# A four-layer attention kernel whose recorded order, engine choices and PSUM banks are replaced by another set

## The chip, the cores and the metric

The kernel runs on one core of one Trainium2 chip. The metric is the device time of one execution in microseconds (us). A core has TensorE (PE in the profile), which multiplies matrices into PSUM, VectorE (DVE), ScalarE (ACT), GpSimd (POOL) and SyncE (SP), which here only issues transfers. Each engine plays its own list of instructions in order and waits on semaphores for the others. PSUM has eight banks; one bank holds 128 partitions by 512 float32.

## What is computed

The input x is [1, 2048, 512] in bf16. Four layers follow one another, each with a layer norm before it and a residual after it: A, B, A, B. There are 32 heads of 16 elements. A is linear attention, B is attention over a sliding window of 256 positions.

```python
def _A_ref(x, wqkv, wo):
    ...
    phi = lambda t: jnp.where(t > 0, t + 1, jnp.exp(t)) + 1e-6
    pq, pk = phi(q), phi(k)
    kv = jnp.einsum("bhsd,bhse->bhde", pk, v)
    z = jnp.einsum("bhsd->bhd", pk)
    num = jnp.einsum("bhqd,bhde->bhqe", pq, kv)
    den = jnp.einsum("bhqd,bhd->bhq", pq, z)[..., None] + 1e-6
    o = num / den
    return (lambda x, *d: x.transpose(*d))(o, 0, 2, 1, 3).reshape(B, S, D) @ wo

def _B_ref(x, wqkv, wo):
    ...
    scores = jnp.einsum("bhqd,bhkd->bhqk", q, k) * (Dh ** -0.5)
    mask = (idx[:, None] - idx[None, :] >= 0) & (idx[:, None] - idx[None, :] < W)
    scores = jnp.where(mask[None, None], scores, -1e9)
    p = _softmax(scores, axis=-1)
    o = jnp.einsum("bhqk,bhkd->bhqd", p, v)
    return (lambda x, *d: x.transpose(*d))(o, 0, 2, 1, 3).reshape(B, S, D) @ wo

x = x + _A_ref(_layernorm(x, axis=-1), A_wqkv, A_wo)
x = x + _B_ref(_layernorm(x, axis=-1), B_wqkv, B_wo)
x = x + _A_ref(_layernorm(x, axis=-1), A_wqkv, A_wo)
x = x + _B_ref(_layernorm(x, axis=-1), B_wqkv, B_wo)
```

## The kernel before

The 2048 rows are cut into 16 tiles of 128 rows. A Python class first writes down a graph of 2532 operations, one operation being one instruction or a short run of matmuls on one engine, with the data that it reads and writes and the PSUM tiles that it uses. The residual stream `xres` stays on the chip for all four layers.

A layer of kind A does, per tile: the norm (bn_stats L330, bn_aggr L331, two small POOL operations L332 and L333, and the normalised tile xn L334); a transpose of xn, either by a DMA (L340, issued from SP) or by TensorE into PSUM with a copy out (L346, L353); the products k and v (L369) and q (L383); phi, which is an exp on ScalarE (L392) and two VectorE operations (L393, L394). In the first layer the sums over the whole sequence are gathered by the operation g (L444), in the third by kv (L423). From these sums come the small matrices M (copied by L358), the denominators den (L506), their reciprocal (recf L510, recb L511), its spread over the rows (L519) and the scaling of q (pqd L526). Then per tile aout (L369 with M) and the residual (L537).

A layer of kind B does, per tile: the norm again, and bq, bk (L383) and bv (L369) from the transposed tile xT; copies out of PSUM (bqe L358 to XQ, bke L554 or L555, bve L358 to vS); two copies of the keys to `kB` by DMA (kd, L563) and two of the values to `vB` (vd, L582), all from SP; scores (L599) with exp on ScalarE (L609) and a mask on VectorE (mk L615); the part of the window that is two tiles away (scores L632, exp L641) with the mask mf, which can run on POOL (L649) or on VectorE (L650); the values product pv (L674), the reciprocal of the sums (rcp L685) and the division (div L686); a transpose of o (oT, by DMA or by TensorE L709), the output product bout (L369, for the last tile L720), and the residual (L537, for the last tile two halves L726). Tiles 0 to 14 of the last layer go out by a DMA from POOL (L783), the last tile by two from SP (L727).

Layer B of tile t needs the tiles around it alone, so neighbouring layers overlap: the front of layer 2 starts while layer 1 ends, and the norm and k of layer 3 run inside layer 2.

What sets the order is no planner that runs at build time, but a recorded table. `TABLE` (L796 to L852) is a compressed string. `place()` unpacks it into three things: one global order of all operations, the engine of each operation, and the bank of each of 997 PSUM tiles. Each engine's instruction list is the global order cut to that engine. Where a PSUM tile takes a bank, its first operation waits for all users of the tile that held the bank before:

```python
order = [ops[raw[2 * k] + 256 * raw[2 * k + 1]] for k in range(n)]
...
o.eng = ("PE", "ACT", "DVE", "POOL", "SP")[raw[2 * n + o.i]]
...
x.banks = [raw[3 * n + k]]
...
before = held[x.banks[0]]
if before:
    assert all(u.t0 < o.t0 for u in before.users)
    o.deps.extend(u for u in before.users if u not in o.deps)
held[x.banks[0]] = x
```

`synchronise()` then turns the dependencies into semaphore waits, with a ring of 48 semaphores for the transfers from SP. `run()` plays the order on each engine. On TensorE it starts with nine matmuls on zeros whose result nobody reads (they go to bank `SPARE`), and `FILL` (L857) puts further ones behind chosen operations: two behind the first, one behind the fourth, six behind the sixth.

Of the kernel before, what the change touches and what calls it, by code (L numbers as in the profile page):

```python
# [11 lines left out]
P = 128  # L12
D = 512
DH = 16
S = 2048
T = 16
# [196 lines left out]
class Plan:  # L213
# [579 lines left out]


TABLE = (
    r"c-rk(1Jq?nlFo<>WR`8)wr$(CZQHhO+qP|2wQYCpd+)ER>6z)7?d|Q|b9PU~|G&KV2EL5=B3_<%jfrF;8#GZ(6a&T@Hqi{3=q9BR6T`$bsZ44U",  # L796
    r"%cL=}O&pWf#5L)Rnmi_+NpJF+_@=$dVDg##CZkDUI+#JGqse3{nyIFk>0}C+X(qENXq-uCN}435kntv|8Emqc#wMKEX_}bCX1SSenwo4TndxkX",
    r"m>Fh;X=b{ZT_(IaZL*uLCWk3yikrgbuIXlSn&zgv*=_EbnI@6xVa}LbW|qlnhMJY;7gNr(Fsn>YGt8VdtIcq8-?TKn%tvO88DYws(xxPwGb7C?",
    r"6B&w_*=CO!ZO)rH=2w&4d~7b52d0l1W9FK@rnebuJ~1!NJ~PjJYSx;EX1-ZxN|<q`j7bXX%_FnGj5h{0n9s~YlMFVRYUXou(PW29X1^(GqQGU7",
    r"!W=N0%@vaz4w_OB6|S1crZhY;Dd3O+Xbgu<4TG@BJT*tmQIis)!58M4Nd>u0eRJJBHx*13^QCEJu9+9+D^tmof#_i2YZC)<Kuz<FA!uzFaza^n",  # L800
    r"$FwoIpd1J^fp1M)lN(ZlLLHL_(m*>?*QAB-jDrZKDWrqSCOyQ2dL|b1HMLD_=x5?Ud8lRjo48N`JWPa&kQWA+d=MWhK~Xc%#Do0M$Yg{JP#Gqe",
    r"MP{)n01Zq*SYir6LsJ+gnn`A<X$F&EnW+jbpbFH5de9MS!(_9?R5w#h9jI!ynodw3wwVUd5E{XD(;1GL=FkOpn3m8Ux<M;w3+<pQw1(rR4RnAT",
    r"=7i}1lVJ*UhovwTmcdDL2ByKg<}56SZE({}hf`(-yl1w<Ot@uMz${n^=U_Ihg73|0m;*bYC%kVKz#7;IYhfWAhudZm?1Emf8&1F;SPXOFB-}Cc",
    r"Afo9FKbXBRAI?J`*attFjnEG^!8-WBEP<cQX1D--;Ua{CQ*a4BH0vQ8{%peIWe5-b;R;m12rvK+!3H=C5g`I@fk$uzDq<vf0!Lv#RKf#r8XiML",
    r"{1C3fRyYVB!$)uzjzJ`>jFIskM8Rut1*771xDTH~G`xzR!&A5cpFkD73D@v5cnDST8C1htFbN;P3#g8h@eX_e@o@@1hZL9quVX5Vj_*JXjDZO;",
    r"B__d`*bozAGQ5F}a4O!0FJT}w#-un62f@4W6*R@^7z<}$226yhF*e@BjF=p6;d_t?;$SAs4DZ8COoLy;Ec^hnKwA6;vfyAyhjlP3WX1IO6V%0Q",
    r"P!qFZW^9J_uogDK7ML9uV{Kf5&G9yN!ljr4?_g)li7oMG$c0_-7s!pRups^lv#~YK!I$t9+u&UM7M`KOt{4vizlXbs_#ETnJ^T(VcEkHP4+(qV",
    r"4=^7KVO#8udGJRljP)@eR)Zqg0INe@EQ;;0J=TB)xB_cJ0w{((u{f^64p;ygYk}ZO?1%}W1S+n<)z}O3<610<z0qMQT!#;^5B9}Gum#uSVBCO-",
    r"VJmLKB(M=ZF2jeo376w$e1t<_JC??wPzIyfvKZYChY?T?ci=E60y{B=9fIX?DDJ|dFbs>qhZxh=wjbectYc%@;TYTQ!H+SH9f8GRFV?jq@mm~)",
    r"`*4AcYrn@55YH~O`|&%hXWzx-_9%XW@8Kdl8sEo$xY$0mi*Skk0Y}18`wrH(&ujxb3I<?*Y-q<|3LD>kfXi%3`y~#<WB4^bw}bFFCa_=O2|R#}",  # L810
    r"?5B7TM?+(~+<t?fVM2QdGuY4ZG5&}zY({$+U*Jjn2{YLz_ywl1@7SMlEWT?O;xCxij>98pZF74HGu!ca8gtn9Y&zS*PQcW5BA&sVHkD0p6WRA|",
    r"V%yT@vU%)T%wm(+y!ISswfSsEo6R<{*=;AA+cvfNE!k$av+ZixcC!Vn*e<raJ&$TH;IG)jUc`bnnSF_uu#LTpZLP6|th0S>Ve4%>8_t%r8*P6J",
    r"c9ZRA2U@i4ZFt+$4zerk0K3`tvV-k5o7DEUrR;V)#73~CZ6CYCma)6+P}{+lwY%*a`++TIciOeKyxn6f*dlhF9cGK#y>_J?ZY$bi_K+Q6E7?`{",
    r"h>d7V*wr?Y9cK^QG4Q1=ZpT7o`<2~lCqOFt+HSF_X*{&D<KURBY+KtX_JmDCRcusS)sD2s?T5CSU2m(~kL(6J+NP!Pc7jbuAKRlgJ)N@??I@dp",
    r"+EWM0NEhrR`-#m&pW2i5yxnIf+p%_vooe^nj`W%R$zHNw*aP;IJ!pTno#?dv#eQec*ex{8cBb#`S-X|G(69Eg%}rzMHu}NlAxn8F8%?)NUFk=g",
    r"ox0IWOLWoZpl__wb~4nR9POaYw3C25Wg(<p^tlx(Kw0UE{ni$ut2P|Xum$OwooS2Ebvw(3r=oPj&bBvg1e#-S*<w_IBGNY$i3(Fi>P^L|58bwv",
    r"s0`h)ed${&OC{(#ia{l*GL@t6X(;ue;gpZcQ&0MVO3{y$pLSCf8b&`+Y3fB)X(UynyS6%wrV(_{)}@~*CXJ$46q)YZ*ffB0QWSb%2hu}(l=e_m",
    r"8brq^4o#)wRF4MJ7@9_LDH_G2TvVSP+4wY_hENT9Y!gsTicSe>u5Cc`Y%MxK4XHmJr1`cEO{9L*hz`+Mnnb_Q6FZI?(+rwSP3RPjr@b_RPSX@h",
    r"MEmFrC8qs!j*?JQnn`Er0yU$gG>ekadAdcj3HT(<q1%Lfkrq*H61IGYu95Nyx<Sq9E;(*N*Xa^nrj~S*!gDKHOjjr(U!^6~nj&yyUP||98Aav$",
    r"w4Czs3W~xHXeGtwhm@Zq@pFp9tLRrMz%MB-&!yF5I62Luc$|WwaU1eHpHfnMK0<9N0WYMpe3;tNIZnur=mjkx=Ew97CE{?rhTf$ow3dk9qxX3o",  # L820
    r"CFc(~I<Kdc{60OS4RoGUa18!{I&n<?kUr$%9E(5V#9We}(#M>HOK@RM%}Kc+cjjbVgwyaf?!wo(D3{{${1I)W3j8q@<4shWEAnP4!-Y5%-{8tz",
    r"mM?H6uFB>3BH!dHe2IJWE$+kB_!GL#pHg4$&T08G>c>6#bNYnS@fXyCKjrjXoj>Cm+>0~taPG?e`Ewr0HTer3z#}*#*Wye(m<MtL&dguZARfx2",
    r"_$$i7mw5<(O<8#<U*Y9k!w%zRT${V`3a)9davdJcb$JXo<gr}KHsXa`pU3fH9?xI$B5ustxE^QcCY*ztGRQ`5#$WMf&dJSr32$PQuek-U<=p%Y",
    r"uj7`yh4b)w{+1_jUf#eHITugj?|3VJ&y#r@ujC*2N1no~cq(t_X}p75@oH|*cX&Fl;TilB-{pI}ldUwD`@D-E@NVA2E#x8Z<<|U&_i-DZ$1}MD",
    r"&*#UypWE^QCOOE5cow(g!#tax@DYB>3z+37pW<UYhv)KfKF!a#BR}U8e3D=A8GeV~<@fk!ZYFspkNm>L<X0{t;ib4lkfQRE3rPtv5>Z47O96=_",
    r"`6RNGl>DMnN(zdT($Z2|Nf~J^V`ZGglr~aUdP^T^E90e|#FF;XSC&W==^*{2qb!w9;w7r|mkBaJVoNs}D9fa~Oq9+tNG3@S2`7VPvUHK2GDPA?",
    r"Ihi6|rI!qqxDri<NqLzn!)1g_laW$EmP<t$CDCQNtdJ_QQpU(CsVp;OmduvXGE*wae5oo6WR9$sW3o{0$Xq!gG32f+lC5%F?#VpaCEMh_ES5bI",
    r"MYqcuiK@Hhft-?u5=}plM{-)CYZ)!8XC#K6lusq5K9&z9mX^~e@|k=t@g%m!m-3oecF0GvRuV`Yt)Tm4uT<1^@`db|N}5nM$a>i+N#uZ>m8bHt",
    r"B$8*6R1V5Uc`lb^lN^#{a#*fNa@i~|<Q+L8Tja7Fl`rL8`9$LCR}xRJ%KLIouE}|cuV2fLazPU4Mfq7OYf`-~-$*k3NfK&uttN@|S4pYW#b_1%",
    r"R=$(8@{7Ebbn?BtCpDz5{vhcEG?k{%dYVB}Yeu;tH>JL&QPEq1npjoSs@1AW>NK6QR@3mBUTdh=>RMAXXf~~-Q#FT9(~KHUhv;<8u8nl4HqlI)",  # L830
    r"Q-^70ZLGsJmqySmnny=yR*k45b(E%%+!{$!%4jX5sU)wC(d?31a!6!NBl)z57S`IDUz=)9X{H6Vffm(F(n1?*X2~T5^|mC@+|pdzX&oJ_?X`op",
    r")Z%(pi|IH$r&*+?bky-$N6za6tt%6?mSmMqI!SBG9__5zWUqG761q=kX-VC$v-NW=rC;bA?W(=Bw0^1eq>oP416p6Y=@dPvy>*@*(yz3YF3`E!",
    r"TEEuA`i*wiBicZ|)%n^++v+m?PSdy*+Cyh(PfhC<Y7_UpF4umV&Rx=`F1@>=i?qM?)n;z7Ue*k5l`heln$aEAmAYCpxutqco4XUbMq9XRdR$w&",
    r"liJGN(5pH?*Xlq$rPp<n4$>d=jBe4J`lGgXr*)lXcAIsu{-pPGz24Vt`m=7(3;IBR(T#dhAL*|O?ul+!bhq@eS|=`xd#Jb7xu?2S^SV2#?yiP&",
    r"`CNGSO!K=o?zu*AwcHD3m({(awOvG)&3&Za?a(?dyL(r6D!KQxo{Qvmsd4XXEca5|x;U<#`%ojh_Aa*T=c2gXn!`nP{asGi)zx*m+yEENb#u|(",
    r"#~Rmtpxxak8p9=WpK1q}$0czcT}+qTeWvkTCzse2a`D|jSJ)+R1zl2C#1(S|TtZjEC3g*_s7vM=NpaU$=C~$O&dqgArMz3~=DBsQf-C8Ix%sY?",
    r">+Ke}^{%vA==!)tu97R`Qn=1;v8&=zy0UJG>+7z#RIaj{<gU7ku8T|Urno`wnj7pUyQ*%RyY8yF?QV!0>Z-dNZil<+M!BA@hP&mQuj$4(?{B-Q",
    r"ZmGND!uio|m|Nz;`w?!MTj6@R<!+@L?l!qqu87~_#=4?@wTs|Kx`_U%tM7KYNPe^1=Zg7f?tmNTwz}tTyxZ?0`*&S&AI0x-@3{%CgrDekyOREW",
    r"SISR!huj`_*X?zOU1@*M9dv7419#sYai`n{_knBZHoDU;sz2%)xoG~3`_?sf(fu*^y*uvCxd-k$cf!5nzH}$uL-)d+bzi#~?!0^CX1cH3hi;aO",
    r";XiVZ-48CN|Hj4jv)#uomjBho^Do^e?nhU~$M-)u<J0+{T^#?Z`^9DO=s$DmeIgG&f&bi9^<TKeKB2$hF1n2ViA&;>`Ag3FYCeT8>#O^6KDJNp",  # L840
# [12 lines left out]
)

FILL, SPARE = {1: 2, 4: 1, 6: 6}, 6  # L857


class Kernel(Plan):  # L860
# [153 lines left out]
```

## Time and profile before

| | us |
|---|---|
| median of four runs | 431.83 |
| lowest, highest | 431.75, 433.44 |
| the profiled execution | 431.78 |
| its span in the trace | 430.1 |
| outside the span | 1.68 |

The mean granted TensorE clock was 0.988 of full speed. The page cuts the span into 40 slices of 10.75 us; each digit is a busy share in tenths:

```profile
PE   8899999999899999999999999999899989998775
DVE  6998898998998799897887789988798687966474
ACT  2433547999899999999998255999999988999992
POOL 4789221101240233130403303212144414242000
PEclk9999999999999999999999999999999979999989
```

Layer 1 lies in about the first seven slices, layer 2 up to about slice 21, layer 3 in slices 20 to 27, where ScalarE is emptier, and layer 4 in the rest. In the clock's row a 9 is full speed; in two places, slice 33 and slice 39, it is lower. The costliest groups are read in this way: line, engine, operation, output and input with their shape, count; then busy time and the mean of one in ns; then the idle time of the engine just before them and what ended it.

```profile
L609 ACT ACTIVATE pb<-ps 128x1024 bf16<-128x1024 f32 (+2 forms) x224 | 207.2, 1041 | 8.9 <-PE ps L599 7.6
L674 PE MATMUL ps<-vB,pb 128*128 128x34 bf16 x2560 | 83.7, 178 | 2.5 <-DVE pb L615 0.6
L383 PE MATMUL ps<-xT,wBp 128*128 128x128 bf16 x1024 | 69.6, 219 | 2.2 <-DMA xT<-xn 1.5
L649 POOL TENSOR_SCALAR_AFFINE_SELECT pb<-pb 128x1024 bf16<-128x1024 bf16 x30 | 35.2, 1174 | 38.8 <-ACT pb L641 37.6
```

The exponentials of the scores are by far the largest group: 224 instructions of about a microsecond, 207.2 us on ScalarE, which sat idle for 8.9 us before them.

### The profile page before, as it was taken

The page shows a single profiled execution, that of the slowest core. Times are in us where ns is not written, and L with a number is a line of the kernel's source. Part 1 is how long each engine was busy: PE and PEld are TensorE (multiplying, and loading weights), DVE is VectorE, ACT ScalarE, POOL GpSimd, SP SyncE. Part 2 cuts the span into 40 slices and gives each one's busy share as a digit, 9 for nine tenths or more (in the row PEclk, how much of TensorE's full clock was granted, in tenths as well). Part 3 has the DMA queues.
Part 4 walks back from the last instruction along what each step waited for, and adds up shares of the span by engine and source line. Part 5 has one row for each costly group of instructions (what it writes and reads, how often), then busy time and mean ns, then how long its engine had stood idle before and what let it go on. Part 6 is the DMA issues. An engine that isn't in the chain of part 4 may idle for free.

```text
span 430.1 us, 17112 instructions
## 1 busy us (share of the span) xinstructions
PE 402.4 (94%) x7548; PEld 257.7 (60%) x7548; DVE 355.9 (83%) x796; ACT 347.5 (81%) x433; POOL 128.3 (30%) x223
## 2 busy tenths in 40 slices
PE   8899999999899999999999999999899989998775
PEld 3445676766465566565566768576657636665444
DVE  6998898998998799897887789988798687966474
ACT  2433547999899999999998255999999988999992
POOL 4789221101240233130403303212144414242000
PEclk9999999999999999999999999999999979999989
DMA  8833016433152533452315000552423622553321
GB/s 247 265 76 87 2 40 161 117 93 74 38 106 63 103 101 76 93 114 53 99 41 66 15 2 29 122 107 64 113 77 95 111 76 65 98 141 107 79 53 50
DMA packets 66978, 37.81 MB, mean 88 GB/s; under 512 B 48248, under 2 KB 61816, under 8 KB 66904
## 3 DMA queue, kind: packets, MB, share of 16 engines
q1 hardware_dynamic: 66176, 34.75, 35.0%
q0 software_dynamic: 720, 1.97, 1.3%
q8 instruction: 59, 0.97, 1.0%
q14 instruction: 15, 0.12, 0.1%
q10 hardware_dynamic: 8, 0.00, 0.0%
HBM read 6.29 MB, written 2.10 MB: 20 GB/s over the span
## 4 chain that ended last, share of the span: by engine, by line
PE 43%; ACT 33%; DVE 15%; DMA 4%; issue 3%; POOL 1%; SPq 0%; POOLq 0%; ACTq 0%
ACT pb L609 23%; PE ps L369 15%; PE ps L383 11%; PE ps L674 7%; ACT pb L641 5%; PE ps L599 5%; ACT vp L609 3%; DVE XQ L526 2%; DMA xT<-xn 2%; DVE stats L330 2%; DVE vp L394 2%; PE ps L444 1%; DVE tE L393 1%; DVE vp L334 1%; ACT tE L392 1%
## 5 line engine op out<-in xcount | busy, mean ns | idle before, releaser
L609 ACT ACTIVATE pb<-ps 128x1024 bf16<-128x1024 f32 (+2 forms) x224 | 207.2, 1041 | 8.9 <-PE ps L599 7.6
L674 PE MATMUL ps<-vB,pb 128*128 128x34 bf16 x2560 | 83.7, 178 | 2.5 <-DVE pb L615 0.6
L674 PEld LDWEIGHTS ps<-vB,pb 128*128 128x128 bf16 x2560 | 77.9, 96 | 13.5 <-issue 3.0
L392 ACT ACTIVATE tE<-ps 128x512 bf16<-128x512 f32 x64 | 39.0, 612 | 41.0 <-PE ps L369 20.7
L383 PE MATMUL ps<-xT,wBp 128*128 128x128 bf16 x1024 | 69.6, 219 | 2.2 <-DMA xT<-xn 1.5
L332 POOL TENSOR_SCALAR ve<-mv 128x1 f32<-128x1 f32 x64 | 16.5, 259 | 175.7 <-DVE mv L331 173.9
L383 PEld LDWEIGHTS ps<-xT,wBp 128*128 128x128 bf16 x1024 | 58.8, 98 | 14.8 <-issue 3.8
L615 DVE TENSOR_TENSOR pb<-pb,tri 128x512 bf16<-128x512 bf16 x112 | 48.0, 436 | 12.4 <-ACT pb L609 11.6
L599 PE MATMUL ps<-XQ,kB 32*128 32x256 bf16 (+2 forms) x1024 | 50.2, 271 | 8.2 <-ACT pb L609 3.9
L369 PE MATMUL ps<-wA,XQ 128*128 128x512 bf16 x192 | 49.3, 380 | 1.7 <-DVE vp L394 1.0
L641 ACT ACTIVATE pb<-ps 128x1024 bf16<-128x1024 f32 x50 | 49.3, 1057 | 0.9 <-PE ps L632 0.8
L537 DVE TENSOR_TENSOR xres<-ps,xres 128x512 bf16<-128x512 f32 x63 | 43.0, 685 | 7.7 <-PE ps L369 6.8
L649 POOL TENSOR_SCALAR_AFFINE_SELECT pb<-pb 128x1024 bf16<-128x1024 bf16 x30 | 35.2, 1174 | 38.8 <-ACT pb L641 37.6
L330 DVE BATCH_NORM_STATS2 stats<-xres 128x6 f32<-128x512 bf16 x64 | 43.1, 681 | 2.7 <-DMA xres<-in_A_x_dram 2.1
L333 POOL TENSOR_TENSOR rs<-ve,negh 128x1 f32<-128x1 f32 x64 | 37.5, 586 | 5.3
L369 PE MATMUL ps<-wBv,xT 128*128 128x512 bf16 x128 | 36.4, 389 | 0.6 <-ACT pb L609 0.4
L599 PEld LDWEIGHTS ps<-XQ,kB 32*128 32x128 bf16 x1024 | 15.5, 92 | 35.8 <-ACT pb L609 15.4
L369 PE MATMUL ps<-M,XQ 128*128 128x512 bf16 x128 | 35.3, 389 | 1.4 <-DVE XQ L526 1.3
L383 PE MATMUL ps<-XQ,wA 128*128 128x128 bf16 x512 | 36.1, 219 | 0.2 <-DVE vp L394 0.2
L383 PEld LDWEIGHTS ps<-XQ,wA 128*128 128x128 bf16 x512 | 30.6, 98 | 7.7 <-DVE vp L394 1.2
L369 PE MATMUL ps<-wBo,oT 128*128 128x512 bf16 x124 | 33.1, 382 | 0.8 <-ACT pb L609 0.6
L685 DVE RECIPROCAL rc<-ps 128x16 f32<-128x16 f32 x64 | 16.1, 252 | 17.0 <-PE ps L674 16.6
(109 smaller groups left out, 541.5 us busy)
## 6 DMA issues: line engine op xcount, KB each, us to landing
vB<-vS SPq DMA_DIRECT2D x64, 136.0 KB, 2.6
kB<-vp SPq DMA_DIRECT2D x64, 128.0 KB, 2.3
out_dram<-xres POOLq DMA_DIRECT2D x15, 128.0 KB, 2.6
wA<-in_A_wqkv_dram SPq DMA_DIRECT2D x3, 512.0 KB, 5.7
xres<-in_A_x_dram SPq DMA_DIRECT2D x2, 512.0 KB, 4.9
pb<-in_B_wqkv_dram SPq DMA_DIRECT2D x1, 1024.0 KB, 8.3
xres<-in_A_x_dram SPq DMA_DIRECT2D x3, 256.0 KB, 4.7
wAo<-in_A_wo_dram SPq DMA_DIRECT2D x1, 512.0 KB, 7.1
```

What stands on the lines that cost most here:

```text
L330: self.on("DVE", "stats", lambda e: e.bn_stats(K.stats[:, t, :], K.xres[:, t, :]), key, dve(512), rd=[("xres", t)], wr=[("stats", t)])
L333: self.pow = self.on("POOL", "pow", lambda e: e.tensor_tensor(K.rs[:, t, :], K.ve[:, t, :], K.negh[:], ALU.pow), key + 0.03, (640, 690), r ...
L369: m = e.matmul(K.ps(ps), lhs(c), rhs(c), start=c == 0, stop=c == 3)
L383: m = e.matmul(K.ps(ps)[:, f * P:(f + 1) * P], w(c, f), xT(c), start=c == 0, stop=c == 3)
L392: self.on("ACT", "E", lambda e: e.activation(K.tE[:, s, :], K.ps(ps), ACT.Exp, bias=0.0), key, act(512), wr=[("tE", s)], ps=[ps])
L537: self.on("DVE", "res", lambda e: e.tensor_tensor(K.xres[:, t, :], K.ps(po), K.xres[:, t, :], ALU.add), key, dve(512), rd=[("xres", t)], w ...
L599: m = e.matmul(K.ps(ps[gq])[:, ns * i:ns * i + ns], K.kB[rows, j % 4, 2 * f + b, :, :], K.XQ[rows, f, q:q + ns], start=True, stop=True, ti ...
L609: return e.activation(out(2 * h, 2, ns), i, ACT.Exp, bias=0.0, scale=0.25)
L615: return e.tensor_tensor(x, x, K.tri[:, 0, :].unsqueeze(1).unsqueeze(1).to_broadcast([P, 4, n, 64]), ALU.mult)
L641: return e.activation(far(h), i, ACT.Exp, bias=0.0, scale=0.25)
L649: return e.affine_select(out=x, in_=x, compare_op=ALU.is_ge, fill=0.0, base=-2, pattern=[[0, 16], [-2, 64]], channel_multiplier=1)
L674: m = e.matmul(K.ps(ps)[:, 34 * u:34 * u + 34], K.P((b // 2) % rp)[:, gq, f, o:o + P], K.vB[:, (b // 2) % 4, b % 2, r, :], start=i == 0, s ...
```

## The change

The operations, their dependencies through data and all instructions that compute are the same. The recorded table is another one, so that all of its lines differ, and one filling matmul is added behind the eighth operation of TensorE:

```diff
 TABLE = (
-    r"c-rk(1Jq?nlFo<>WR`8)wr$(CZQHhO+qP|2wQYCpd+)ER>6z)7?d|Q|b9PU~|G&KV2EL5=B3_<%jfrF;8#GZ(6a&T@Hqi{3=q9BR6T`$bsZ44U",
...
+    r"ALN64kPq@fK8P{@22lJcMg",
 )
...
-FILL, SPARE = {1: 2, 4: 1, 6: 6}, 6
+FILL, SPARE = {1: 2, 4: 1, 6: 6, 8: 1}, 6
```

Unpacked, the two tables differ as follows. "Moved" counts the operations that have another place among those which stay on their engine.

| engine | operations before | after | moved | farthest |
|---|---|---|---|---|
| TensorE | 858 | 858 | 179 | 10 places |
| VectorE | 795 | 797 | 338 | 17 places |
| ScalarE | 432 | 429 | 46 | 1 place |
| POOL | 219 | 220 | 70 | |
| SP | 228 | 228 | 124 | 5 places |

Of 997 PSUM tiles 117 have another bank. 24 operations change engine: eight masks mf go from VectorE to POOL and seven from POOL to VectorE; two bqe and one xT copy (L353) go from VectorE to ScalarE; one ge, two ve, two oTe (all copies out of PSUM) and one recb go from ScalarE to VectorE.

The moves on TensorE are dense in its first 130 operations (the first 60 us), around its operations 470 to 560 (about 230 to 267 us) and in its last ten. Single places that the text below speaks of, with the times that the operations had before:

- Opening: the normalised tile 3 goes ahead of a bn_stats on VectorE.
- Near 55 us: a transpose by TensorE goes behind a q.
- Near 116 us: an aout goes ahead of scores.
- At 139 us on SP: the transpose goes ahead of a copy of values (vd) that was ahead of it.
- Near 267 us: a bq has another bank (4 before, 3 after), which one of the pqd used before it, and it is put behind a bk.
- Near 270 us on SP: the transposes of layer 4's first tiles go ahead of kd and vd.
- Near 301 us on SP: two kd go ahead of the transpose that was issued at 301.51; on POOL one output goes behind a mask.
- Near 348 us: one mask goes from POOL to VectorE, and the mask goes ahead of the reciprocal and the division.
- Near 405 us: scores go behind a pv.
- At the end: bout and residual of tile 14 go ahead of the last tile's second half and its residuals.

## The prediction

> **What bounds the kernel now.** I read the page first (busy shares, slices, chain), then a table of windows, then the timeline wherever neither TensorE nor ScalarE is saturated.
>
> ```profile
> PE 402.4 (94%) x7548; PEld 257.7 (60%) x7548; DVE 355.9 (83%) x796; ACT 347.5 (81%) x433; POOL 128.3 (30%) x223
> PE 43%; ACT 33%; DVE 15%; DMA 4%; issue 3%; POOL 1%; SPq 0%; POOLq 0%; ACTq 0%
> ```
>
> The average says TensorE, the chain says two owners in turn. The windows (duration, then busy PE, PEld, DVE, ACT, POOL, clock, DMA share, GB/s) separate them:
>
> ```profile
> 15.00:20.00 5.00, 3.88 (x19) 1.26 (x17) 5.00 (x13) 1.58 (x3) 4.04 (x11) 1.00 1.04 292
> 20.00:84.00 64.00, 62.16 (x779) 38.73 (x779) 58.97 (x129) 34.89 (x53) 28.89 (x53) 1.00 0.34 79
> 134.00:190.00 56.00, 53.82 (x1084) 33.04 (x1083) 49.12 (x112) 53.41 (x63) 17.34 (x27) 1.00 0.43 93
> 206.00:290.00 84.00, 83.06 (x1488) 56.99 (x1488) 71.86 (x162) 61.65 (x88) 20.59 (x33) 1.00 0.28 57
> 301.00:313.00 12.00, 10.15 (x209) 6.91 (x207) 9.36 (x21) 11.33 (x15) 1.33 (x2) 1.00 0.38 101
> 340.00:356.00 16.00, 13.91 (x236) 7.40 (x234) 12.50 (x23) 13.20 (x16) 5.98 (x8) 0.80 0.30 84
> 356.00:421.00 65.00, 58.17 (x1422) 38.99 (x1420) 45.18 (x104) 64.68 (x76) 15.46 (x22) 0.97 0.37 92
> ```
>
> 20 to 84 and 206 to 290 us belong to TensorE (97% and 99% busy), 356 to 421 to ScalarE's exponentials (64.68 of 65.00). An order can't shorten a full engine. What it can win are the seams: VectorE full at 15 to 20; 0.4 to 0.8 us holes near 116 and 143; 1.85 us of PE idle at 301 to 313; 2.09 at 340 to 356; and the tail. These holes add to about 8 us, and most have a dependency behind them.
>
> The timeline at three seams (start, duration, engine; the bracket is idle time before, and its releaser):
>
> ```profile
> 143.61 1.05 PE L383 MATMUL ps<-xT,wBp 128*128 128x128 bf16 x16 [0.52 <-DMA xT<-xn]
> ...
> 306.95 0.61 PE L383 MATMUL ps<-xT,wBp 128*128 128x128 bf16 x8 [1.02 <-DMA xT<-xn]
> ...
> 349.64 0.61 PE L519 MATMUL ps<-rec,spread 32*128 32x128 bf16 x16 [0.78 <-DVE o L686]
> 351.06 1.03 PE L369 MATMUL ps<-M,XQ 128*128 128x512 bf16 x2 [0.80 <-DVE XQ L526]
> 352.69 1.94 ACT L609 ACTIVATE vp<-ps 128x1024 bf16<-128x1024 f32 x2 [1.52 <-PE ps L599]
> ...
> 425.33 0.88 DVE L726 TENSOR_TENSOR xres<-ps,xres 128x256 bf16<-128x256 f32 x2 [1.47 <-PE ps L720]
> 425.78 0.84 SPq L727 DMA_DIRECT2D out_dram<-xres  x2
> 426.19 0.69 DVE L537 TENSOR_TENSOR xres<-ps,xres 128x512 bf16<-128x512 f32 x1
> 427.18 0.54 POOL L783 DMA_DIRECT2D out_dram<-xres  x1 [7.45 <-DVE xres L537]
> ```
>
> The last output leaves from POOL at 427.18; it waits for tile 14's residual (L537, 426.19 to 426.88), which stands behind tile 15's two half residuals (L726).
>
> **What the Trainium skill says.** "TensorE: Matmul & The Clock Gate", Part 1, "What's actually happening": the clock is full or half, set by TensorE's activity in free-running windows of 3413 ns. Agrees: the windows show 0.50 from 350 to 356, matmuls that take 0.38 us on average last about 0.5 each there. The page ties the drop to an idle window; here the waits before it are only 0.49, 0.78 and 0.80 us, so its trigger isn't settled by this trace. "Trainium Kernel Development and Optimization", "Key Constraints": transfers of all queues share 16 DMA engines and interleave. Agrees: the transposes awaited at 143.61 and 306.95 take 4.36 and 5.30 us (139.12, 301.51), other copies 2.3 to 2.6. "PSUM — Partial Sum Buffer", "PSUM bank collisions raise a hardware error": guard PSUM by bank. The program does: the first instruction on a bank waits for all users of the tile before it, so a changed bank number changes waits.
>
> **The change part by part.** Same 2532 operations; 24 change engine, 117 of 997 PSUM tiles change bank. On each engine the movement is small: PE 179 of 858 operations (at most 10 places), ScalarE 46 by one place each, DVE 338 of 784 (at most 17), POOL 70, SP 124 (at most 5). So I price neighbourhoods.
>
> - Added warm-up matmul after TensorE's eighth operation: one of about 0.22 us, in TensorE's wait for a transposed tile near 11.2 us. 0; if the cover is gone +0.2.
> - Opening, 0 to 20: a normalised tile goes ahead of a bn_stats (0.68 us), so a transpose starts about 0.8 earlier, but VectorE is full (5.00 of 5.00) and the next k groups wait for its phi behind the same work. 0, bounds -0.4 and +0.4.
> - 55 to 69: a PE transpose goes behind a q group (some 0.45 us); bk, its copy and the kB transfer follow, and the first scores at 68.9 wait for that transfer. Slack hides part: +0.2 (0 to +0.45).
> - 116: aout goes ahead of scores that wait 0.79 us for exp; but ScalarE is full from 117 on. -0.1 (0 to -0.25).
> - 139 to 145, SP queue: the transpose issued at 139.12 stood behind a vB copy (L582, 0.60 us of issue). Now it precedes it: 0.6 earlier, against a PE hole of 0.52 and a ScalarE hole of 0.40 at 145.09. The vB copy behind it isn't needed until the values. -0.4 (0 to -0.5).
> - Engine changes: 8 masks DVE to POOL, 7 back (0.71 us on DVE, 1.17 on POOL); four copies to DVE and one xT copy and two bq copies to ScalarE (0.6 to 0.7), two oT copies (0.38) and a recb. VectorE's sum changes by under 1 us. Near 147 two masks (1.4 us) come before pqd, just fitting before the spread at 148.4, and a 0.6 us copy on ScalarE lies in its 0.8 us hole at 150. At 247 both neighbours have room (ACT idle 12.97 of 25 between 230 and 255). 0; +0.7 if the masks do delay pqd.
> - 267: a bq group's bank was changed, so it now waits for one of the four pqd (0.61 us each, 267.16 to 269.62). With old times it would come up to 2.6 us late, 0.8 if its pqd, itself moved earlier, runs first; bk is put before it as filler. TensorE is full here, so what it waits is lost: +0.3 (0 to +0.8).
> - 269 to 279: transposes before kB and vB copies on SP; slack 7 us or more, TensorE full. 0.
> - 301 to 311: the transpose issued at 301.51 lands after 5.30 us beside two output copies from POOL; now one output goes behind a mask, and two kB copies go far ahead. PE's 1.02 shrinks, but exp near 308 and pqd at 309.25 come next. -0.4 (0 to -0.8).
> - 340 to 356: a mask leaves POOL for DVE (+0.7 on DVE) and the division precedes others differently; the spread at 349.64 is then gated by exp, at about 349.4. -0.2 (+0.5 to -0.3). The half clock is priced under the rivals.
> - 353 to 421: no operation enters or leaves ScalarE's queue; exps of two neighbours swap at 405. +0.1 (0 to +0.3).
> - Tail: tile 14's bout and residual go ahead of tile 15's residuals: 14's residual 0.6 us earlier, its POOL output with it; 15's outputs then land about where 14's did less 0.1 to 0.5. Masks on POOL cost 0.46 each with 0.6 slack. -0.5 (0 to -0.6).
>
> Sum: 0.2 - 0.1 - 0.4 + 0.3 - 0.4 - 0.2 + 0.1 - 0.5 = -1.0. The profiled execution is 431.78 (span 430.1 and 1.68 around it), 0.05 below the median; 431.78 - 1.0 = 430.8.
>
> **The rivals.**
> Seams close and the half clock goes with them (B). The half-speed window pair of 6.83 us follows the three waits of 348.5 to 351.1. If the earlier spread shortens them, the doubled matmuls (1.03 for a pair, against about 0.8) and ScalarE's idle 1.52 and 1.28 us at 352.69 and 355.91 go, some 2 us. For: it is the largest hole left. Against: only 0.2 of about 2 us of waiting is removed, and the windows run free. 430.8 - 2.0 = 428.8.
>
> New waits on VectorE's reordered queue (C, slower). One mechanism: an in-order VectorE now serves pqd, divisions and phi in an order that releases banks later, and TensorE, at 97 to 99%, has nothing to lay over it. Places where the new order with old times leaves an operation later than its consumer: bq at 267 (up to 2.6), division at 124.5 (up to 1.6 past its slack), bout and scores at 403 to 406 (1.0, 0.9), k at 99.3 (0.6): 6.7 us together, of which most is absorbed because the predecessors move too. If 1.0 stays as PE holes and they bring one more half-speed window (3.41 us of work at half: 1.7 lost), +2.7: 433.5. It decides from 2.3 us on (the 1.0 gained plus 1.3). For: 338 VectorE moves, engine at 83%. Against: most moves are swaps with slack.
>
> Nothing (D): fillers meet the saturated engine next, each gain is taken back at the next wait: 431.8. For: 97 to 99% stages everywhere. Against: nothing follows the tail.
>
> **How the numbers follow.** About 0.3%, 1.3 us, is what can be told from no change. A (430.8, own range 429.8 to 432.0) 0.38; B 0.18; C 0.34; D 0.10. Faster (under 430.5): 0.17 of B and 0.13 of A, 0.30. Slower (over 433.1): 0.30 of C. Same: the rest, 0.40. The range 428.6 to 434.6 takes in B and C with the unknown bounds (-1.0 and the absorbed part of C) and leaves about 2 in 10 outside. Cases of both signs hold most; A's own range stands beside it.
>
> **What would show it.** Right: no PE wait of 0.5 near 143; the 306.95 hole under 0.6; tile 14's residual before tile 15's and POOL's last issue near 0.6 us earlier relative to the last values; DVE's sum within 1 us of 355.9; TensorE's busy time as before in 206 to 290. B: clock 1.00 where the last-but-one layer's end stands now at 350 to 356. C: new PE holes with DVE pqd, div or phi as releaser in 84 to 134 or 255 to 290, or a third half-clock place. Wrong altogether: a loss or gain over 1 us in a full stretch, which would mean that stages thought saturated had hidden waits.

## The result and the profile after

The changed kernel took 434.22 us (median of 43 runs, 431.08 to 439.2), the kernel before beside it 431.62 (64 runs, 430.01 to 435.8). The ratio is 1.0054, with a 95% interval of 1.0041 to 1.0067: slower by about 0.5%. The profiled execution of the changed kernel took 433.27 us, its span is 431.5.

Three lines of its page: busy shares, the chain by engine, and the granted clock in 40 slices.

```profile
PE 401.5 (93%) x7549; PEld 257.8 (60%) x7549; DVE 358.7 (83%) x798; ACT 345.8 (80%) x430; POOL 131.5 (30%) x224
PE 44%; ACT 27%; DVE 19%; POOL 5%; DMA 3%; issue 2%; SPq 0%; POOLq 0%; ACTq 0%
PEclk9999999999999999999999999999999989999889
```

TensorE and ScalarE have no more work than before; VectorE is busy 2.8 us longer (358.7 against 355.9) and POOL 3.2. New in the chain is POOL with 5%, where it had 1%, and there is one more dip of the clock near the end. The windows say where (duration, then busy PE, PEld, DVE, ACT, POOL, clock, DMA share, GB/s):

```profile
20.00:84.00 64.00, 60.26 (x728) 37.43 (x727) 58.44 (x124) 32.33 (x50) 29.53 (x56) 1.00 0.36 78
301.00:313.00 12.00, 10.52 (x218) 7.57 (x213) 9.74 (x23) 11.74 (x16) 3.74 (x5) 1.00 0.36 90
340.00:356.00 16.00, 13.85 (x257) 8.01 (x255) 12.39 (x23) 14.59 (x16) 6.08 (x6) 0.89 0.41 95
```

From 20 to 84 us TensorE is busy for 60.26 us instead of 62.16, while the seams at 301 and 340 are fuller than before (ScalarE 11.74 and 14.59 against 11.33 and 13.20). So the loss sits in the stretch from 20 to 84 us, which had looked saturated.

Since both programs have the same operations, each can be matched with itself. This table gives how much later TensorE's operations end than the same ones in the profiled execution of before (us; median over those that ended, before, in the 8 us from the time in the first column on; where operations change places, single ones lie up to about 1 us from the median). It is worked out from the traces of the runs told below, one execution each.

| at | changed | open_before | open_after | pool_open | early_before | front_before | after_copies | after_far | before_far |
|---|---|---|---|---|---|---|---|---|---|
| 16 | 0.01 | 0.57 | 1.29 | 1.53 | 0.04 | 0.87 | 1.11 | -0.15 | 0.32 |
| 24 | -0.01 | 0.61 | 2.58 | 2.48 | 0.21 | 2.40 | 2.43 | -0.15 | 0.24 |
| 40 | 1.00 | 0.57 | 2.91 | 2.59 | 0.43 | 2.71 | 2.43 | 0.10 | 1.82 |
| 72 | 1.80 | -0.20 | 5.49 | 2.50 | 0.86 | 2.94 | 3.09 | -0.54 | 1.42 |
| 136 | 2.01 | 0.00 | 5.48 | 2.70 | 1.07 | 3.15 | 3.29 | -0.35 | 1.42 |
| 144 | 1.50 | -0.51 | 5.33 | 2.19 | 0.56 | 2.63 | 2.78 | -0.86 | 1.38 |
| 296 | 1.82 | -0.18 | 5.31 | 2.51 | 0.88 | 2.96 | 3.13 | -0.32 | 1.45 |
| 312 | 1.25 | -0.75 | 4.76 | 1.95 | 0.31 | 2.39 | 2.55 | -0.89 | 1.91 |
| 352 | 0.50 | -3.68 | 3.93 | 0.34 | -0.56 | -0.65 | 0.75 | -1.56 | 1.86 |

The changed kernel loses 1.8 us between 32 and 72 us. It wins back 0.5 at 139 to 144, of which 0.3 is gone again by 296, and 0.6 at 301 to 312. It loses 0.4 up to 340 and wins 1.2 from there to 352, where one half-speed window of 3.41 us (a stretch in which the granted clock is 0.50) stands in place of two. Later it loses 0.7 in a half-speed window at 417.4, and some at the tail.

The 1.8 us begin like this in the changed kernel's timeline (start, duration, engine, operation; the bracket is idle time before, with its releaser):

```profile
33.42 1.19 DVE L334 TENSOR_SCALAR vp<-xres,mv,rs 128x512 bf16<-128x512 bf16 x1 [0.20 <-POOL rs L333]
33.44 1.02 POOL L311 MEMSET vS<- 128x1106 bf16 x1
...
35.37 0.67 POOL L333 TENSOR_TENSOR rs<-ve,negh 128x1 f32<-128x1 f32 x1
...
36.07 0.93 DVE L334 TENSOR_SCALAR vp<-xres,mv,rs 128x512 bf16<-128x512 bf16 x1 [0.45 <-POOL rs L333]
...
37.65 0.55 PE L467 MATMUL ps<-ones,vp 128*128 128x1 bf16 x16 [0.91 <-DVE vp L394]
```

and the same norm before, where the memset had run 2 us earlier, beside another norm's last step:

```profile
31.20 1.03 POOL L311 MEMSET vS<- 128x1106 bf16 x1
31.23 1.15 DVE L334 TENSOR_SCALAR vp<-xres,mv,rs 128x512 bf16<-128x512 bf16 x1
...
34.51 0.69 POOL L333 TENSOR_TENSOR rs<-ve,negh 128x1 f32<-128x1 f32 x1
...
35.24 0.92 DVE L334 TENSOR_SCALAR vp<-xres,mv,rs 128x512 bf16<-128x512 bf16 x1
```

POOL's memset now stands ahead of a norm's power (L333), which starts at 35.37 instead of 34.51. VectorE has the norm's last step (L334) in its queue ahead of a phi, so the phi is late too, and TensorE waits 0.91 us for it. It waits another 0.60 us for a phi at 44.91 and 0.92 for a transposed tile at 68.82. Before had none of these three; its longest wait there is 0.77 at 68.89, for a copy of keys. That is a story from one execution, which ended 1.5 us later than before's; the medians ask for 2.6.

### The profile page after: what moved, and what is told of

Its sections match the earlier page's. It is cut to its first block, busy times and chain, and to the rows that moved or that the text cites. A ratio compares the mean times of both kernels' runs of the same rounds, so it can differ in the third digit from the quotient of the medians.

```text
span 431.5 us, 17121 instructions
## 1 busy us (share of the span) xinstructions
PE 401.5 (93%) x7549; PEld 257.8 (60%) x7549; DVE 358.7 (83%) x798; ACT 345.8 (80%) x430; POOL 131.5 (30%) x224
## 4 chain that ended last, share of the span: by engine, by line
PE 44%; ACT 27%; DVE 19%; POOL 5%; DMA 3%; issue 2%; SPq 0%; POOLq 0%; ACTq 0%
ACT pb L609 18%; PE ps L369 16%; PE ps L383 10%; PE ps L674 9%; ACT pb L641 5%; PE ps L599 5%; DVE XQ L526 3%; DVE stats L330 3%; DVE xres L537 3%; DVE XQ L394 2%; ACT vp L609 2%; POOL rs L333 2%; DVE tE L393 1%; DVE vp L394 1%; DMA xres<-in_A_x_dram 1%
## 5 line engine op out<-in xcount | busy, mean ns | idle before, releaser
L615 DVE TENSOR_TENSOR pb<-pb,tri 128x512 bf16<-128x512 bf16 x112 | 49.1, 445 | 12.5 <-ACT pb L609 11.7
L369 PE MATMUL ps<-wA,XQ 128*128 128x512 bf16 x192 | 50.5, 380 | 1.1 <-DVE vp L394 0.5
L649 POOL TENSOR_SCALAR_AFFINE_SELECT pb<-pb 128x1024 bf16<-128x1024 bf16 x31 | 38.2, 1234 | 40.2 <-ACT pb L641 38.8
L333 POOL TENSOR_TENSOR rs<-ve,negh 128x1 f32<-128x1 f32 x64 | 37.6, 587 | 5.3
L369 PE MATMUL ps<-wBv,xT 128*128 128x512 bf16 x128 | 36.8, 389 | 0.6 <-ACT pb L609 0.4
L369 PE MATMUL ps<-wBo,oT 128*128 128x512 bf16 x124 | 34.3, 389 | 2.7 <-DMA oT<-o 1.5
L369 PE MATMUL ps<-M,XQ 128*128 128x512 bf16 x128 | 35.0, 386 | 1.2 <-DVE XQ L526 1.2
```

What stands on the lines that cost most here:

```text
L333: self.pow = self.on("POOL", "pow", lambda e: e.tensor_tensor(K.rs[:, t, :], K.ve[:, t, :], K.negh[:], ALU.pow), key + 0.03, (640, 690), r ...
L369: m = e.matmul(K.ps(ps), lhs(c), rhs(c), start=c == 0, stop=c == 3)
L615: return e.tensor_tensor(x, x, K.tri[:, 0, :].unsqueeze(1).unsqueeze(1).to_broadcast([P, 4, n, 64]), ALU.mult)
L649: return e.affine_select(out=x, in_=x, compare_op=ALU.is_ge, fill=0.0, base=-2, pattern=[[0, 16], [-2, 64]], channel_multiplier=1)
```

## The experiments

Ratios are to the kernel before on the same chips, with 95% intervals. "Changed" is the changed kernel.

| run | median | ratio | interval |
|---|---|---|---|
| changed | 434.22 | 1.0054 | 1.0041 to 1.0067 |
| open_before | 430.82 | 0.9990 | 0.9970 to 1.0010 |
| open_after | 437.01 | 1.0119 | 1.0095 to 1.0143 |
| pool_open | 433.42 | 1.0040 | 1.0023 to 1.0057 |
| after_nofill | 434.28 | 1.0054 | 1.0029 to 1.0080 |
| early_before | 432.91 | 1.0052 | 1.0034 to 1.0069 |
| norms_before | 434.94 | 1.0096 | 1.0058 to 1.0134 |
| front_before | 432.63 | 1.0032 | 1.0012 to 1.0052 |
| middle_after | 431.01 | 0.9988 | 0.9962 to 1.0014 |
| after_loads | 433.55 | 1.0045 | 1.0022 to 1.0068 |
| before_loads | 434.71 | 1.0057 | 1.0037 to 1.0077 |
| mixed_loads | 432.20 | 1.0024 | 1.0004 to 1.0043 |
| tail_after | 432.31 | 1.0010 | 0.9988 to 1.0032 |
| after_far | 430.49 | 0.9975 | 0.9955 to 0.9994 |
| before_far | 432.56 | 1.0022 | 1.0003 to 1.0041 |
| mixed_far | 432.26 | 1.0016 | 0.9997 to 1.0035 |
| after_copies | 433.65 | 1.0050 | 1.0030 to 1.0070 |
| far_old_tail | 430.77 | 0.9975 | 0.9958 to 0.9991 |

### Which stretch loses

The two global orders hold the same operations up to many positions, so one table can be spliced into the other. `OTHER` is the other kernel's table, `raw` now holds it, and `CUTS` says which stretch takes its order, engines and banks:

```diff
+    for lo, hi in CUTS:
+        part = order[lo:hi]
+        inside = set(part)
+        order[lo:hi] = [o for o in other if o in inside]
+        for o in part:
+            engine[o.i] = raw[2 * n + o.i]
+        for k, x in enumerate(tile_of):
+            if x.users[0] in inside:
+                bank[k] = raw[3 * n + k]
```

open_before, the changed kernel with `CUTS = [(0, 439)]`:

> The changed kernel with the kernel before's order, engines and banks in the first 439 operations (up to about 71 us) and without the added filling matmul. In the profiles the changed kernel loses 1.8 us between 32 and 64 us. Theory (the opening is the cause): this run comes back by about 1.8 us of the 2.3 to 2.6 lost, so 0.4 to 0.8 us over the kernel before (432.0 to 432.4 against 431.6). Rival (new waits of VectorE and the banks in the later layers): it stays at 433.5 or more.

open_after, the kernel before with the same cut:

> The complement: the kernel before with the changed kernel's first 439 operations and its added filling matmul. Theory (the opening): about 1.8 us slower than before, 433.4. Rival (later layers): 431.6 to 432.0.

middle_after, the kernel before with `CUTS = [(439, 2511)]`:

> The kernel before with the changed kernel's operations 439 to 2511 (about 71 to 421 us): the opening and the tail stay as before. Theory (the middle gains what was priced there, about -0.5 at 139 and -0.4 at 301, and the tail loses 0.2 to 1): 430.2 to 430.8, a little under the run with the old opening and the new tail. Rival (middle and tail are a wash): 431.4 to 431.8.

tail_after, the kernel before with `CUTS = [(2511, 2532)]`:

> The kernel before with the changed kernel's last 21 operations (from 421.7 us on). The prediction put the new tail at -0.5. In the changed kernel's profile tile 14's output product waits 1.08 us for its transposed tile ahead of tile 15's transpose, and tile 15's outputs are issued last. Theory (that wait is passed on to the last tile): 0.2 to 0.9 slower than before. Rival (the prediction's): 0.3 to 0.6 faster.

The opening is what loses: with the old one the loss is gone altogether (0.9990, more than the 1.8 us that the theory gave back), alone it costs 1.19%. The new middle is worth 0.12%, and its interval holds 1; the new tail 0.10% the other way, which holds 1 too, so neither's theory is settled. The middle's interval ends at 1.0014, under the 1.0054 to be explained, so the rival of late waits in the later layers falls. One thing doesn't add up: the opening alone costs more (5 us, in only six runs) than the whole change (2.6). The traces offer a reason in the next part: what the opening costs is not the same in each execution.

after_nofill takes the added filling matmul away:

```diff
-FILL, SPARE = {1: 2, 4: 1, 6: 6, 8: 1}, 6
+FILL, SPARE = {1: 2, 4: 1, 6: 6}, 6
```

> The changed kernel without the added filling matmul. Theory (the filling matmul lies in a wait of TensorE): within 0.2 us of the changed kernel. Rival (it delays the first products or keeps the clock up): 0.2 to 0.5 us faster, or slower by a half-speed window's cost of about 1.

No difference shows. But the interval is 1.1 us wide to either side, so a cost of some tenths would not be seen.

### What in the opening loses

pool_open moves the memset of the timeline above behind the power:

```diff
+    order.remove(ops[80])
+    order.insert(order.index(ops[310]) + 1, ops[80])
```

> The changed kernel with one POOL operation put back: the memset of vS (about 1.03 us) that stands ahead of the pow of a norm near 35 us goes behind it; every other engine's list is the changed kernel's. Theory (the POOL queue holds up the norm, and the phi behind that norm on VectorE): the pow ends about 0.8 us earlier, the phi that TensorE waited 0.90 us for at 37.6 comes 0.6 to 0.9 earlier, and the whole is 0.6 to 0.9 faster than the changed kernel. Rival (TensorE's and ScalarE's new order in the opening): no more than 0.2 us.

By the medians it is 0.8 us faster than the changed kernel, as the theory said, but the two intervals overlap. In its trace the 1.8 us between 24 and 72 us are gone (2.48 and 2.50 in the table). That does not show that the POOL queue made them, since this execution was 2.5 us late before that stretch began. after_nofill is late in the same way and has the memset where the changed kernel has it. Its power starts at 36.50, that of pool_open at 35.40, but the wait for the phi differs by 0.2 us only (0.64 at 39.60 in pool_open, 0.84 at 39.73 in after_nofill), and the changed kernel's wait at 44.91 is absent from both.

What made pool_open late stands further ahead. Here are the chain of waits, the timeline and two windows of it; the chain's line is start, duration and what. A run's line numbers are shifted by the lines that its edit adds, so that L371 here is L369 above:

```profile
15.73 5.93 DMA XQ<-vp
```

```profile
21.70 1.89 PE L371 MATMUL ps<-wA,XQ 128*128 128x512 bf16 x4 [1.62 <-DMA XQ<-vp]
```

```profile
18.00:21.50 3.50, 1.62 (x7) 0.40 (x5) 3.50 (x12) 0.95 (x2) 2.86 (x7) 1.00 0.92 112
21.50:24.90 3.40, 3.20 (x8) 1.20 (x9) 1.34 (x5) 0.60 (x1) 2.71 (x8) 0.50 0.46 80
```

The transpose of tile 5, issued on SP at 15.73, takes 5.93 us. TensorE waits 1.62 for it, and in the half-speed window that follows its matmuls take nearly twice as long (four take 1.89 us, where four take 1.04 in the run below). With the old opening the same wait is short, as open_before's timeline shows:

```profile
20.95 1.04 PE L384 MATMUL ps<-wA,XQ 128*128 128x512 bf16 x4 [0.33 <-DMA XQ<-vp]
```

At the same time a 1 MB weight load (8.3 us on the page of before) is under way. Measured from that load's landing, the transpose has two places to land, and none between. The wait is TensorE's idle time before the products that need the transpose:

| run | issued | after the load landed | wait of TensorE |
|---|---|---|---|
| before, open_before, early_before, middle_after, tail_after | 15.95 to 16.68 | 0.42 to 0.49 | 0.27, 0.33, 0.57, none, 0.96 |
| changed | 15.99 | 0.43 | none |
| norms_before | 15.75 | 0.50 | 1.11 |
| pool_open, after_nofill, open_after, front_before, after_copies | 15.57 to 15.84 | 1.86 to 1.88 | 1.62, 1.84, 2.50, 1.76, 2.21 |

With the old order of the first 155 operations it was early in five executions of five, with the new order late in five of seven; and the profile on which the result was first read was one of the two lucky ones. So no trace of the changed kernel itself shows the late landing; after_nofill, which differs from it by one filling matmul, does. The wide spread of the changed kernel's times (431.08 to 439.2, against 430.01 to 435.8) fits a loss that comes and goes. The early landing is no full protection either: in norms_before the load itself landed late, at 20.66, and the execution was 2.2 us late by 32 us. A second transpose, beside the 512 KB load near 65 us, shows the same: 0.48 to 0.52 us after that load in all five executions with the old order there, 1.91 to 2.33 in three of seven with the new. In open_after TensorE waited for it, and another half-speed window followed:

```profile
71.40 1.05 PE L398 MATMUL ps<-xT,wBp 128*128 128x128 bf16 x16 [1.98 <-DMA xT<-xn]
```

```profile
72.50:75.90 3.40, 3.40 (x26) 1.88 (x25) 1.22 (x2) 2.67 (x3) 0.00 (x0) 0.50 0.52 131
```

Three splices into the changed kernel, `[(0, 155)]`, `[(155, 330)]` and `[(330, 439)]`, asked for the parts.

early_before:

> The changed kernel with the order of before in its first 155 operations alone (to about 24 us) and without the added filling matmul. In the profiles with the changed kernel's opening the transpose of tile 5, issued near 15.7 us beside the last weight load, landed 1.9 us after that load in three of four and brought a half-speed window at 21.5; with the opening of before it landed 0.5 us after the load in both. Theory (the early part sets which of the two landings is taken): 0.5 us after the load, no half-speed window before 60 us, and a median 1 to 2 us below the changed kernel's (432.2 to 433.2), with the wait for the norm at 35 to 38 us still there. Rival (the landing is chance, the loss is the POOL queue's from 30 us on): 434 or more.

norms_before:

> The changed kernel with the order of before in its operations 155 to 330 alone (about 24 to 53 us), where the memset stands behind the norm's pow and the exps of the fourth q and k are in their old order. Theory (two losses that hide each other): where the transpose of tile 5 lands late this gains little, so the median is 0.3 to 1.2 us below the changed kernel's. Rival (the POOL queue and the order of the norms are the whole loss): 1.8 or more below, 432.4 or less. Second rival (nothing lies here): within 0.3.

front_before:

> The changed kernel with the order of before in its operations 330 to 439 alone (about 53 to 71 us), where a transpose by TensorE was put behind a q and a key copy ahead of a value copy on SP. Theory (losses before 53 us): within 0.4 us of the changed kernel. Rival (the order here makes the transpose beside the last weight load land late, and a half-speed window follows at 72.5): 1 to 2 us below the changed kernel.

Each alone gives little: 1.0052, 1.0096 (six runs) and 1.0032, where all three together give 0.9990. The median of early_before fell where the theory put it, but its ratio did not move, and the ratio decides: missed. norms_before came out slower than the changed kernel, which none had said. The median of front_before fell where its rival put it, but the interval overlaps that of the changed kernel. The half-speed window at 21.5, which the first of these texts gives to all three late executions, was in two of them only; open_after waited longest and had none there. The traces agree with losses that hide each other: early_before has no late transpose but still loses 0.65 us between 24 and 72; front_before is 2.4 us late at 24 us and then loses only 0.5 more.

### Taking the loads away from the transposes

after_loads, before_loads and mixed_loads (old opening and tail, new middle) issue the two loads a little later:

```diff
+    for a, b in ((11, 168), (13, 477)):
+        order.remove(ops[a])
+        order.insert(order.index(ops[b]) + 1, ops[a])
```

> The changed kernel with the two last weight loads later on SP, and nothing else moved: the 1 MB load of layer 2's weights goes behind the transpose of the eighth issue place (near 19 us instead of 11.5), the 512 KB load of its output weights goes behind the value copies near 75 us instead of 63.5. Theory (the late landing of the two transposes beside these loads is most of the opening's loss): the transpose of tile 5 lands under 3.5 us after its issue, no half-speed windows at 21.5 or 72.5, and the median falls 1.5 to 3 us below the changed kernel's, to 431.2 to 432.7. Rival (the loss is the order of POOL and VectorE between 30 and 60 us): the transposes land earlier, but the median stays above 433.5.

> The same two loads moved in the kernel before. Theory: its transposes landed 0.5 us after the loads, so less is to be had: 0.3 to 1.0 us below before (VectorE is full at 15 to 20; the first scores at 68.9 waited for a key copy of 4.7 us beside the load). Rival (before isn't held by these landings): within 0.2. Against both: the load of layer 2's weights lands near 24 us beside other transposes and makes those late, 0.5 slower.

> The old opening and tail, the changed kernel's operations 439 to 2511, and the two loads moved: the version that should beat both if the gains add. Theory: 0.5 to 1.5 us below before (ratio 0.9965 to 0.9988). Rival (each gain is taken back at the next full engine): within 0.3 of before.

The transpose of tile 5 now came 2.5 us after its issue, but the one issued at 20.76 in before_loads had the load beside it, which landed at 26.46: the transpose landed at 26.97, and TensorE waited 2.0 us for it. The load was moved onto another victim, and all three were slower than before, against the theory of each.

So the loads went where SP issues nothing, between 42 and 59 us. The POOL copies that unpack the first of them have to follow:

```diff
+    moves = [(11, 12), (13, 11)] + list(zip((84, 91, 85, 88, 89, 90, 87, 86, 94), (83, 84, 91, 85, 88, 89, 90, 87, 86)))
+    order.remove(ops[83])
+    order.insert(order.index(ops[81]) + 1, ops[83])
+    for a, b in moves:
+        order.remove(ops[a])
+        order.insert(order.index(ops[b]) + 1, ops[a])
```

after_far does this to the changed kernel, before_far to the kernel before, mixed_far to the splice of middle_after. after_copies is the changed kernel with the POOL part alone, the loads left where they were. far_old_tail is after_far with the old last 21 operations.

> The changed kernel with the two last weight loads in SP's empty stretch of 42 to 59 us, behind the load of the value weights, and the eight POOL copies that unpack the first of them (0.76 us each) with the memset that waits for them behind the other constants, where layer 2's weights are still ready before 57 us. So no transpose of layer 1 or of layer 2's front has a big load beside it, and eight copies leave the POOL queue between 28 and 42 us. Theory (the opening's loss is these two things): every transpose of the first 40 us after the fourth weight load lands 2.4 to 2.9 us after its issue, the wait of 0.90 for a phi near 37.6 goes, and the median is 2 to 4 us below the changed kernel's, 430.2 to 432.2, near what the same edit makes of the kernel before. Rival (the new order on TensorE and ScalarE itself): 433 or more.

> The same edit in the kernel before. Theory: it had less to lose there, so 0.3 to 1.5 us below before, and the changed kernel with this edit differs from it by no more than 1 us. Rival: within 0.3 of before.

> The same edit with the old opening and tail and the changed kernel's operations 439 to 2511. Theory: the lowest of the three, 0.5 to 2 us below before. Rival: no different from the edit in the kernel before, so that the new middle is worth nothing.

> The changed kernel with the POOL half of the last edit alone: the eight unpacking copies and their memset go behind the other constants, and the weight loads stay where they are. Theory (two causes that hide each other: late transposes and the POOL queue): the pow that came at 36.04 comes under 34, but the transposes beside the loads can still land late, so the median lies between the changed kernel and the full edit: 0.5 to 2 us below the changed kernel's (432.2 to 433.7). Rival (POOL is the whole cause): 430.5 to 431.2, as with the full edit. Second rival (the loads are the whole cause): no gain, 434 or more.

> The changed kernel with the full edit (loads and copies moved) and the last 21 operations in the old order. Theory (the new tail costs 0.2 to 0.6): 0.1 to 0.6 below the changed kernel with the full edit, a ratio to before of 0.996 to 0.998. Rival (the tail is worth nothing either way, or the half-speed windows decide): no different from it.

after_far keeps every new order of TensorE, ScalarE and VectorE and goes from 1.0054 to 0.9975: 430.49 us, faster than both kernels. So these orders do not lose by themselves; they lose with the loads and copies where they were. Its theory held for the time but not for all transposes: the one of tile 5 took 2.8 us, the next two 3.8 and 3.9, without a load beside them. after_copies parts the halves: its power ended at 35.41 instead of 36.04 (not under 34, since this execution was late already), the transpose landed late (1.87), and the ratio stayed at 1.0050. So moving the copies alone gives nothing that shows, and moving the loads as well gives the rest, 0.75%. That the POOL queue costs more where no transpose is late is what the traces suggest; no run shows it. far_old_tail is no different from after_far, so the tail is worth nothing that can be measured.

before_far missed: slower than before (1.0022), where a gain was expected; mixed_far, whose interval holds 1, shows no gain either. The timeline of before_far shows a likely reason, at 36 to 38 us:

```profile
35.51 0.29 DVE L399 TENSOR_SCALAR tE<-tE 128x512 bf16<-128x512 bf16 x1 [1.50 <-ACT tE L398]
...
36.00 1.16 DVE L399 TENSOR_SCALAR tE<-tE 128x512 bf16<-128x512 bf16 x1 [0.19 <-ACT tE L398]
36.06 1.99 POOL L327 MEMSET pb<- 128x1024 bf16 x2
```

The same VectorE operation takes 0.29 us alone and 1.16 beside a POOL memset. With the copies gone, POOL's memsets moved up beside this one and the next, and TensorE waited 0.99 us at 38.84 for the phi behind them. It had waited 0.62 at 32.49 behind another such pair, and the two make most of the 1.82 at 40 us in the table. No run put these memsets elsewhere.

## Why the prediction was wrong

The forecast was 430.8, within 0.3% of before; measured were +0.54%, about 2.3 to 2.6 us. The slower rival gave 433.5, near the time, but that was luck: its mechanism was to act after 84 us, and from 80 to 290 us the lateness of the changed kernel moved by 0.5 at most and ended where it began (1.80 and 1.82), and the middle as a whole is 0.9988 of before. Its sign of a third half-clock place came (352.5, 400.3 and 417.4 us), but the window at 417.4 cost 0.7, where 1.7 was said.

The step that failed is the opening, priced at 0 with bounds of 0.4 on either side, and what it rested on: "20 to 84 and 206 to 290 us belong to TensorE ... An order can't shorten a full engine." It can't, but it can empty one, and the sum had no term for that. What the runs show in its place is a cost of 1.19% for the new opening alone, and none of the loss with the old one. The prediction had named the sign itself, "a loss or gain over 1 us in a full stretch", and 1.8 came there. Its signs of being right came too at the seams: no wait over 0.33 us near 143, the hole at 306.95 down to 0.43, tile 14's output 0.7 earlier after the last values. They could not tell, because none of them looked at the opening. Three things were left out of the sum.

- The opening's bullet looks at tile 3, whose transpose is TensorE's and did come earlier (13.12 instead of 13.64 us). The DMA transpose of tile 5 behind it was not looked at. In five of seven executions with the new order it landed 1.9 us after the weight load beside it instead of 0.5, and TensorE's operations were 2.4 to 2.7 us late by 24 us. The note on shared DMA engines was in the prediction (the Trainium skill, "Trainium Kernel Development and Optimization", "Key Constraints"), and applied to two transposes at 139 and 301 us, but not to these.
- POOL's 70 moves were counted and not priced between 24 and 60 us. In the changed kernel's execution the wait behind the memset was 0.91 us; between two late executions, with the memset ahead of the power and behind it, the difference was 0.2. What it costs where no transpose is late was not tested.
- VectorE beside POOL: durations were taken from the row's mean, while L334 takes 0.40 alone and 1.19 beside the memset. Before paid the same for another tile (1.15 at 31.23), so the memset's place matters here and not its being there. The Trainium skill's "GPSIMD Engine Reference", "1. Specifications", says that the two share their interfaces to SBUF, with contention for some VectorE instructions; the traces show the size, not whether this instruction is of the kind that the page means.

The other steps, by the table of lateness in the changed kernel: 139 to 145, -0.4 said and -0.5 found, most of it gone again by 296; 301 to 311, -0.4 and -0.57; 267, +0.3 and 0.0; 116, -0.1 and +0.2, the wrong way; the added matmul 0, as far as its run can tell; 55 to 69 can't be read, since the medians scatter there by more than the 0.2 said. VectorE's sum, "under 1 us", grew by 2.8. 340 to 356 was -0.2 and came to -1.2, since one half-speed window took the place of two: half of rival B happened, which another execution needn't repeat (open_before and front_before show no such window there, before_far two). B's reading was off in two places: the window pair begins at 349.48, ahead of the last of the three waits that it was to follow, and a pair of such matmuls takes about 0.6 us at full clock (0.59 at 426.08 in the changed kernel), not 0.8. The tail was -0.5; from the end of the last values product to the end of the span the changed kernel takes 7.22 us (424.33 to 431.55), before 6.95 (423.11 to 430.06), and the timing of the tail alone shows nothing. The lines of the changed kernel say where the gain went:

```profile
425.53 0.61 PE L369 MATMUL ps<-wBo,oT 128*128 128x512 bf16 x2 [1.08 <-DMA oT<-o]
...
428.04 0.84 SPq L727 DMA_DIRECT2D out_dram<-xres  x2
```

Tile 14's product waits 1.08 us for its transposed tile while tile 15's transpose, ready to run, stands behind it; tile 15's outputs, issued at 428.04, are last now. The term had carried over tile 14's gain and not tile 15's delay.

What stays open: why a transpose beside a load takes the early or the late landing. All six executions that issued tile 5's at 15.95 or later had it early, five of the six that issued it at 15.84 or earlier had it late; the moment of issue does not decide alone (15.75 early in one run, 15.79 and 15.84 late in others). No run held this transpose back and changed nothing else, and five against seven executions are few. Why the opening alone costs more than the whole change is open with it; in the one trace of open_after both transposes were late.

## What to carry to other kernels

An engine that is 97% busy is a reason to look for what keeps it fed, not to write its stretch off: small moves on the queues that feed it (SP, POOL) can empty it. Where short transfers that others wait for share the DMA engines with a large load, try the load in a stretch without them before tuning any order; here that, with the copies behind the load, turned a loss of 0.5% into a gain of 0.25%, while the same edit cost the kernel before 0.2%, so an edit of this kind is measured on each order anew. One profile may be a lucky one: compare its time with the median, and look at several profiles before pricing a transfer by its landing.

## What was not expected of the hardware

A DMA transpose beside a load landed 0.42 to 0.52 us or 1.86 to 2.33 us after the load, with nothing between, for both loads (1 MB and 512 KB) in the twelve executions that had them in their first places. Without a load beside it the transpose of the third tile of layer 2 took 2.4 us, against 4.0 to 6.0 with it.

A VectorE tensor_scalar on 128x512 bf16 that ran beside a POOL memset ended about 0.14 us after that memset did, and took 1.16 instead of 0.29 us, or 1.19 instead of 0.40. This holds in the kernel before as well (1.15 at 31.23).

In these twelve executions TensorE waited 1.6 to 2.5 us for a late transpose eight times. A half-speed window of 3.41 us followed four times (1.62 in pool_open, 1.84 and 2.38 in after_nofill, 1.98 in open_after) and not the other four (1.76 in front_before, 2.06 in norms_before, 2.21 in after_copies, 2.50 in open_after). So the length of one wait does not decide it.
